# Loading wq with eight strided DMAs of 16 partitions in place of one DMA of 128, in a decode-step transformer block

## The chip, the cores and the metric

The kernel runs on one core of a Trainium2 chip. The metric is the device time of one execution in microseconds (us). Before the change the median of 3 runs is 203.08 us (203.05 to 203.18).

A core has five instruction streams. PE (TensorE) multiplies matrices, DVE (VectorE) and ACT (ScalarE) work element by element, POOL (GpSimd) builds constants here, and SP (SyncE) issues DMAs. A DMA moves bytes between device memory (HBM) and the on-chip buffer SBUF, which has 128 partitions (rows). Sixteen DMA engines share the work of each load. An instruction that needs a load waits on that load's semaphore.

## What is computed

One token goes through one transformer block: attention over a cache of 4096 positions with 32 heads of 128, then a gated MLP, each behind a layer norm and with a residual. All inputs are bf16.

```python
h  = x + A(layernorm(x))
h2 = h + B(layernorm(h))
# A: q = (x @ wq) as 32 heads of 128; scores = q . k_cache / sqrt(128); p = softmax(scores)
#    o = p . v_cache; result = o (4096 values) @ wo
# B: (gelu(x @ w_gate) * (x @ w_up)) @ w_down
# x: 640; wq: 640 x 4096; k_cache, v_cache: 32 x 4096 x 128; wo: 4096 x 640
# w_gate, w_up: 640 x 1728; w_down: 1728 x 640
```

Every weight and both caches are read once: 84.23 MB, of which the caches are 67.1 MB and wq is 5.24 MB.

## The kernel before, in words

**Program order.** The kernel is a list of operations for each engine, with the operations that each waits for written out by hand. `Prog.op` (line 50) appends one, `Prog.dma` (58) appends a DMA, `emit` (63) gives each DMA a semaphore of its own, which reaches 16 when the load has landed, and `_run` (90) writes the instructions with their waits. Each engine runs its list in order. `P.emit({"sync": 2})` (573) puts the first two operations of SP's list ahead of the barrier at which the engines meet at the start, so these two DMAs go out first; the rest of the list follows behind the barrier.

**The loads.** All long loads are issued by SP, in this order: wq (line 186), three cache loads (210), the other cache loads as their buffers come free, three loads of wo, and nine loads of w_gate, w_up and w_down (451 to 468). x alone (1.2 KB) comes from ACT's queue (185). Line 59 is the line of every DMA in the profile.

wq goes into the tile `arena`, 128 partitions of 20,480 elements. Its 640 rows are seen as 128 groups of five, `"(p c) n -> p (c n)"`, so partition p takes one run of 40,960 B from HBM. Later wo takes the same tile, when the q projection has read wq.

The caches come in 16 groups, K and V for G = 0 to 7, four heads each: 128 partitions of 32 KB, 4.19 MB. They go through three buffers (`slots`). Group n waits until the reader of group n - 3 is done (`consumed`, line 206). The last V group comes in two halves.

**The start.** POOL and DVE build constants while the first loads are in flight. x is turned into columns (line 252), normalized (258 to 267) into `xlnB`, and the q projection (line 280; the repeated matmuls have line 28, that of a helper) multiplies it with wq: 40 matmuls, all behind one wait for the whole of wq. The two halves of q are copied to `qb` by DVE (285) and ACT (286). q is needed by the first product on K.

**The groups.** For each group G and each quarter of its K tile, DVE multiplies K by q (`prod`, line 295), PE adds up the products in PSUM (305 and 28), DVE finishes the sums (313) and ACT takes the exponential (317). Then PE multiplies the V tile by these (336 and 28), and DVE and PE pick and collect the heads (353 to 369).

**The end.** The output projection with wo (404), the residual, the second layer norm, gate and up (509), gelu, and down (553), whose last matmuls wait for the last w_down load; four copies (566, 568) and one store.

The functions that the edit touches, with those that call them:

## Time and profile before

| what | us |
|---|---|
| median of 3 runs | 203.08 |
| the profiled execution | 202.97 |
| its span, first to last instruction | 201.7 |
| wq: issue to landing | 15.5 |
| K loads, eight of 4.19 MB: median from issue to landing | 21.0 |
| V loads, seven of 4.19 MB: median from issue to landing | 17.7 |
| first matmul on wq begins at | 15.66 |
| first product on K begins at | 25.25 |
| last load lands at | 199.06 |

How to read the views. All times are from the start of the span. "Busy" of an engine is the time in which it executed something. A row of digits gives the busy share of equal slices in tenths, 9 for 90% or more. The DMA row is the mean busy share of the 16 DMA engines; GB/s is what they moved, booked at the moment when a packet starts, so short slices show bursts. A packet is one row of a load (up to 40 KB here), or the few bytes that each engine writes at the end of its part to count the load's semaphore up. An issue of a DMA is an instruction on SP (SPq); its landing is when its semaphore is complete. Matmul ends are modelled.

### The profile page before, as it was taken

What the parts mean: (1) busy time and instruction counts of PE and PEld (TensorE: products, weight loads), DVE (VectorE), ACT (ScalarE), POOL (GpSimd) and SP (SyncE); (2) the same over time, 40 slices, a digit from 0 to 9 for tenths busy, and PEclk for the clock granted to TensorE, in tenths of its full rate; (3) what the DMA queues carried; (4) which work ended last, traced back from release to release, by engine and by line L of the source; (5) the groups of instructions that cost most, each with busy time, mean ns of one, the idle gap of its engine ahead of it and who ended that gap; (6) DMA issues with size and microseconds to landing.
All of it is one profiled execution on the core that took longest, in us unless ns stands there. A gap on an engine that the chain in (4) does not pass through costs nothing.

```text
span 201.7 us, 1568 instructions
## 1 busy us (share of the span) xinstructions
PE 115.3 (57%) x788; PEld 17.0 (8%) x384; DVE 129.5 (64%) x136; ACT 51.3 (25%) x139; POOL 5.6 (3%) x15
## 2 busy tenths in 40 slices
PE   0108059536737775197529655876396097754564
PEld 0101000000001000000000001001000000121222
DVE  1300188517994898379857966896879979683341
ACT  2100003610560055005502440252025214500111
POOL 7300000000000000000000000000000000000000
PEclk9999756996996699859997978798569859997575
DMA  9999999999999999999999999999999999999992
GB/s 333 439 398 455 442 422 416 416 442 468 432 422 416 416 422 455 443 442 417 416 416 445 442 448 422 422 416 429 442 442 448 387 429 423 427 409 439 415 408 99
DMA packets 4330, 84.32 MB, mean 418 GB/s; under 512 B 482, under 2 KB 868, under 8 KB 1508
## 3 DMA queue, kind: packets, MB, share of 16 engines
q1 hardware_dynamic: 4322, 84.23, 97.9%
q8 instruction: 4, 0.07, 0.1%
q14 instruction: 2, 0.02, 0.0%
q10 hardware_dynamic: 2, 0.00, 0.0%
HBM read 84.23 MB, written 0.00 MB: 418 GB/s over the span
## 4 chain that ended last, share of the span: by engine, by line
DMA 52%; DVE 21%; PE 19%; issue 3%; ACT 2%; SPq 2%
DMA slot<-in_A_k_cache_dram 43%; DVE prod L295 16%; PE bank L28 13%; DMA slot<-in_B_w_down_dram 9%; DVE sc L313 3%; PE bank L336 3%; PE bank L305 2%; ACT p_bd L317 2%; SPq L59 2%; DVE po_r L363 1%; DVE po_m L353 1%; PE bank L553 0%; DVE out_row L566 0%; DVE RT L349 0%; DVE aP L393 0%
## 5 line engine op out<-in xcount | busy, mean ns | idle before, releaser
L295 DVE TENSOR_TENSOR prod<-slot,qb 128x4096 bf16<-128x4096 bf16 x32 | 72.4, 2283 | 24.3 <-DMA slot<-in_A_k_cache_dram 24.3
L317 ACT ACTIVATE p_bd<-sc,zero_t 32x32 bf16<-32x32 f32 x128 | 46.4, 362 | 107.7 <-DVE sc L313 106.5
L28 PE MATMUL bank<-prod,id_b 128*128 128x512 bf16 x224 | 68.6, 458 | 0.0
L305 PE MATMUL bank<-prod,id_b 128*128 128x512 bf16 x32 | 15.3, 477 | 45.2 <-DVE prod L295 45.1
L313 DVE TENSOR_REDUCE sc<-bank 128x32 f32<-128x512 f32 x32 | 22.0, 687 | 14.7 <-PE bank L28 14.7
L336 PE MATMUL bank<-slot,p_bd 128*32 128x512 bf16 x128 | 14.8, 448 | 15.0 <-ACT p_bd L317 13.8
L28 PE MATMUL bank<-slot,p_bd 128*32 128x512 bf16 x128 | 14.9, 453 | 0.0
L305 PEld LDWEIGHTS bank<-prod,id_b 128*128 128x128 bf16 x32 | 3.5, 109 | 108.6 <-DVE prod L295 108.6
L363 DVE TENSOR_REDUCE po_r<-po_m 128x128 f32<-128x1024 f32 x6 | 11.2, 1867 | 0.0
L353 DVE TENSOR_TENSOR po_m<-bank,m 128x1024 f32<-128x1024 f32 x8 | 9.7, 1214 | 0.6 <-PE bank L28 0.6
L280 PE MATMUL bank<-arena,xlnB 128*32 128x512 bf16 x20 | 3.3, 628 | 7.2 <-DMA arena<-in_A_wq_dram 7.2
L285 DVE CAST qb<-bank 128x512 bf16<-128x512 f32 x1 | 0.7, 692 | 10.0 <-PE bank L28 10.0
L336 PEld LDWEIGHTS bank<-slot,p_bd 128*32 128x32 bf16 x128 | 3.8, 106 | 35.7 <-ACT p_bd L317 26.1
L509 PE MATMUL bank<-slot,hlnT 128*1 128x512 bf16 (+1 forms) x40 | 4.0, 486 | 2.7 <-DVE hX L500 2.2
L349 DVE TENSOR_REDUCE RT<-p_bd 128x4 f32<-128x512 bf16 x8 | 5.4, 675 | 0.0
L252 PE MATMUL bank<-one_bf,x_row 1*128 1x1 bf16 x5 | 0.4, 177 | 7.1 <-DMA x_row<-in_A_x_dram 7.1
L369 PE MATMUL bank<-po_r,hs 128*16 128x128 f32 x16 | 3.4, 301 | 1.5 <-DVE po_r L361 1.5
L286 ACT CAST qb<-bank 128x512 bf16<-128x512 f32 x1 | 0.6, 586 | 10.4 <-PE bank L28 10.4
L28 PE MATMUL bank<-arena,xlnB 128*32 128x512 bf16 x20 | 3.2, 613 | 0.0
L404 PE MATMUL bank<-arena,aP 128*1 128x320 bf16 x32 | 2.5, 314 | 1.1 <-DMA arena<-in_A_wo_dram 1.1
L263 ACT ACTIVATE ln<-ln,eps_t 128x1 f32<-128x1 f32 x2 | 0.6, 294 | 9.4 <-DVE ln L261 9.4
L482 ACT CAST A_hi<-bank 97x320 bf16<-97x320 f32 x1 | 0.4, 426 | 9.8 <-PE bank L28 9.8
(87 smaller groups left out, 42.9 us busy)
## 6 DMA issues: line engine op xcount, KB each, us to landing
slot<-in_A_k_cache_dram SPq DMA_DIRECT2D x8, 4096.0 KB, 21.0
slot<-in_A_v_cache_dram SPq DMA_DIRECT2D x7, 4096.0 KB, 17.7
arena<-in_A_wq_dram SPq DMA_DIRECT2D x1, 5120.0 KB, 15.5
slot<-in_A_v_cache_dram SPq DMA_DIRECT2D x2, 2048.0 KB, 14.9
arena<-in_A_wo_dram SPq DMA_DIRECT2D x1, 2560.0 KB, 22.9
slot<-in_B_w_gate_dram SPq DMA_DIRECT2D x1, 2160.0 KB, 11.0
arena<-in_A_wo_dram SPq DMA_DIRECT2D x1, 1920.0 KB, 27.0
slot<-in_B_w_up_dram SPq DMA_DIRECT2D x1, 1296.0 KB, 13.7
```

What stands on the lines that cost most here:

```text
L28: return e.add_instruction(mybir.InstMatmult(name=nc.get_next_instruction_name(), engine=e.engine, start_tensor_calc=start, stop_tensor_ca ...
L59: ev = self.op(eng, lambda e: e.dma_start(out, in_), *deps, dma=True)
L295: m = V(lambda e: e.tensor_tensor(out=prod[:, s % 4, :, :], in0=kt[:, 32 * u:32 * u + 32, :], in1=qb[:, G, :].unsqueeze(1).to_broadcast([1 ...
L305: i = e.matmul(*args, start=True, stop=False)
L313: reds[s] = V(lambda e: e.reduce_sum(sc[:, s % 4, :], ps_f[s % 2][:, :].rearrange("p (g d) -> p g d", d=16), axis=AX.X), folds[s], exps.ge ...
L317: x = A(lambda e, j=j: e.activation(p_bd[32 * j:32 * j + 32, G % 2, 32 * (s % 4):32 * (s % 4) + 32, j], sc[32 * j:32 * j + 32, s % 4, :], ...
L336: return e.matmul(*args, start=(c < 4), stop=(c >= 12))
L349: sums[G] = V(lambda e: e.reduce_sum(RT[:, 4 * G:4 * G + 4], p_bd[:, G % 2, :, :].rearrange("p g j -> p j g"), axis=AX.X), exps[4 * G + 3])
L353: mks[G] = V(lambda e: e.tensor_tensor(out=po_m[:, :, :], in0=po[:, :].rearrange("p (b d) -> p b d", b=8), in1=m8[:, :].unsqueeze(2).to_br ...
L363: evs[G] = V(lambda e: e.reduce_sum(po_r[:, G % 2, :], po_m[:, :, :].rearrange("p b d -> p d b"), axis=AX.X), mks[G], hds.get(G - 2))
L369: return e.matmul(ps_a[0:16, 128 * (G // 4):128 * (G // 4) + 128], hs[:, 12 - 4 * g:28 - 4 * g], po_r[:, G % 2, :], start=(g == 0), stop=( ...
L509: i = e.matmul(po[32 * a:32 * a + 1, 512 * k:512 * k + n], hlnT[:, c:c + 1], w[:, c, 512 * a:512 * a + n], start=(c == 0), stop=(c == 4))
```

## The change

One load of wq becomes eight. Load k takes the 16 partitions k, k + 8, k + 16, ... k + 120 of the same tile from the same rows of HBM, each still one run of 40,960 B. The eight are issued by SP in the order k = 0 to 7, in the place in which the one load stood, and the q projection waits for all eight. The two DMAs ahead of the start barrier are now the loads k = 0 and 1; the first cache load stands behind the barrier. No other operation changes; behind line 186 the line numbers grow by one.

```diff
     d_x = P.dma("scalar", x_row[:, :], A_x[0, :, :])
-    d_wq = [P.dma("sync", arena[:, :], A_wq[:, :].rearrange("(p c) n -> p (c n)", c=5))]
+    wq_v = A_wq[:, :].rearrange("(p c) n -> p (c n)", c=5)
+    d_wq = [P.dma("sync", arena[k:128:8, :], wq_v[k:128:8, :]) for k in range(8)]
     order = [(kind, G) for G in range(NG - 2) for kind in "KV"] + [(kind, G) for kind in "KV" for G in (NG - 2, NG - 1)]
```

## The prediction, made before the changed kernel ran

> **What bounds the kernel now.** I read the page first, for what is busy all the time.

> ```profile
> span 201.7 us, 1568 instructions
> PE 115.3 (57%) x788; PEld 17.0 (8%) x384; DVE 129.5 (64%) x136; ACT 51.3 (25%) x139; POOL 5.6 (3%) x15
> ...
> DMA  9999999999999999999999999999999999999992
> ...
> q1 hardware_dynamic: 4322, 84.23, 97.9%
> ```

> No compute engine passes 64%, while the 16 DMA engines work in every slice but the last; SP's queue alone fills 97.9% of them. The kernel is one stream of loads. Next I cut the span into stages, to see whether the stream has a gap anywhere (columns: stretch, its length, busy time of each engine, clock, DMA share, GB/s).

> ```profile
> 0.00:15.50 15.50, 0.95 (x7) 0.77 (x7) 2.46 (x14) 1.87 (x3) 5.59 (x15) 1.00 0.98 402
> 15.50:25.20 9.70, 4.35 (x40) 0.87 (x20) 0.69 (x1) 0.59 (x1) 0.00 (x0) 0.90 1.00 432
> 25.20:64.40 39.20, 25.12 (x130) 2.21 (x42) 26.55 (x20) 11.58 (x32) 0.00 (x0) 0.81 0.99 428
> ...
> 177.60:199.10 21.50, 11.97 (x191) 5.59 (x157) 8.68 (x29) 1.91 (x5) 0.00 (x0) 0.72 0.95 393
> 199.10:201.70 2.60, 0.70 (x16) 0.31 (x16) 0.63 (x2) 0.57 (x2) 0.00 (x0) 0.50 0.00 0
> ```

> There is none. After the last landing at 199.1 only 2.6 us are left, so whatever the stream loses comes out at the end in full. Does a freed slot ever hold up a load, so that a delay could be absorbed there? The page gives 21.0 us from issue to landing for the K loads and 17.7 for the V loads, where a 4.19 MB load by itself needs 4.19 / 0.433 = 9.7 us. So at every issue some 8 to 11 us of older loads are still ahead; SP is never late, and nothing in the middle can take up a delay.

> Last I look at the DMA part of the stretch in which wq alone is moving.

> ```profile
> DMA  9900399900399900399300799003999003999003
> GB/s 1560 624 0 0 156 936 936 473 0 0 156 1092 780 468 0 0 156 1092 1092 156 0 0 312 1560 624 0 0 156 936 936 468 0 0 156 1092 780 468 0 0 156
> DMA packets 113, 4.55 MB, mean 433 GB/s; under 512 B 1, under 2 KB 2, under 8 KB 2
> ...
> q1 hardware_dynamic: 111, 4.55, 100.0%
> ```

> This is 3.3 to 13.8 us in 40 slices. GB/s are booked where a packet starts, and they come in bursts seven times in 10.5 us, one each 1.5 us: the 16 engines start a row of 40 KB together, take 1.5 us over it, and start the next together. 40,960 B in 1.51 us is 27.1 GB/s for each engine and 433 for all. The same view of K and V loads (45 to 65 us, rows of 32 KB) has 437, of the weights (177 to 188 us, rows of 1.3 to 20 KB) 422. One rate for every row length and every tensor: the sources don't set it. What sets it is either the engine's own speed or the way into SBUF that it writes through. In this kernel each long load covers all 128 partitions, so the trace can't tell the two apart, and on that the prediction turns.

> **The change part by part.**

> *Bytes and rows.* 128 rows of 40 KB stay 128 rows of 40 KB: 5.243 MB, or 5.243 / 0.433 = 12.1 us of the stream. Nothing is removed.

> *Issues on SP.* Seven are added. The trace has 0.33 to 0.61 us for one. The first two instructions of SP go out ahead of the start barrier: until now wq at 0.00 and K0 at 0.44, now wq's first two loads. The other six follow from 1.26 us, at 0.43 each until 3.9, and K0, V0 and K1 move from 0.44, 1.26 and 1.64 to about 3.9, 4.3 and 4.7. Each load of wq keeps the engines for 1.5 us, over three times its issue; the third goes out at 1.26 and is needed at 4.8, and K0 is needed at 13.9. Cost 0, hidden by the rows in flight; were an issue to take longer than a row, the stream would stand still for the difference at each of the six. No other instruction of SP waits for anything new.

> *Completion packets.* The page counts 482 packets under 512 B, 16 for each of SP's 30 big loads and 2 more; now 7 × 16 = 112 are added. No view prices one by itself. Nothing is the lower bound: 45 to 65 us holds 32 of them and runs at 437, wq's stretch holds one and runs at 433. Upper bound: the stretch 177 to 188 has 75 and loses 3% of 11 us against 437, 0.4 us, so 0.6 us for 112 if all of that were theirs. I take 0.1, near the first row, which has the long rows that wq has too.

> *Waits.* PE's first wq matmul waits for eight loads in place of one. Its weights are ready at 10.08 us and wq at 15.66, so the waits lie in idle time of PE, and only the last landing counts. Queued behind are PE's folds, and they wait for K0 (25.2) anyway: from wq's landing to both halves of q takes 5.1 us (15.66 to 20.74), leaving 4.5 us. If wq is late, K0 in the same queues is late by as much, and the 4.5 stays. x lands at 7.08 between rows of wq; with rows of 3 us it may come some 5 us later and the weights at 15, still ahead of wq.

> *Where the rows go.* This is the one large term. Until now a load names all 128 partitions. Each new load names sixteen, k, k + 8, ... k + 120, and as all engines run in step, these sixteen are written at the same time, for k = 0 to 7 in turn. If the engines' own speed is the limit, the price is 0. If it is the ways into SBUF, and numbers eight apart come back to the same ways, then two rows share one and each goes at half of 27.1 GB/s: wq needs 24.2 us in place of 12.1, 12.1 more. If four share, it is 36.3 more. On the side of gains there is next to nothing, since no stretch of the trace is above 437. I take the half: full rate is shown here for the spread over 128 partitions alone, the stream is deaf to everything on the side of the source, and a comb with teeth eight apart is regular enough to meet any regular share-out of partitions over ways unevenly; of the unequal outcomes two on one way is the mildest. 0 and +12.1 are the ends that I keep for the range. One deduction: by the DMA view of 0.9 to 4.1 us the first rows start spread over 0.8 us (1.0 to about 1.8), and while only one of two sharers is running it has the full rate; half of that spread, 0.4 us, comes off.

> [...]

> **Sum.** 12.1 − 0.4 + 0.1 = +11.8 us. The profiled execution took 202.97 (span 201.7 and 1.3 around it), 0.1 under the median of 203.08; 202.97 + 11.8 = 214.8, or 214.9 on the median. I give **214.8**, with 213.3 to 215.8 if only this case's terms are off.

> **Rivals.**

> *Not slower: the engine is the limit, or each row goes to the engine that already owns its way.* Then wq's last row still lands at 15.5, eight issues hide as above, and the time stays 203.1. For it: the row time of 1.51 us is so even that a fixed engine speed explains it well. It needs no sharing at all; the deciding point is whether a row of the first loads takes 1.5 us or 3.0. [...] I give it 0.15, 0.02 of that for a gain above 0.2% (0.4 us, what a measurement of this kernel can tell from no change).

> [...]

> [...]

> *More than double.* Four rows on one way, or losses at each change between two rows: up to +36.3, 239. 0.04.

> **Chances.** Forecast 0.73, not slower 0.15, half 0.08, more 0.04. Faster by over 0.2%: 0.02; within: 0.13; slower: 0.85. The range goes from the half price (209.0, less 0.2) to the top of the forecast, 208.8 to 216.0, and holds 0.81.

> **What would show it.** In the DMA view of wq's stretch: bursts 3.0 us apart and a mean near 217 GB/s, with the DMA share still near 1 (a packet that waits for its way counts as busy). PE's first wq matmul at about 27.4 in place of 15.66, DVE's first product at 37.0 in place of 25.25, later stages as long as before, the last landing near 210.9 and 2.6 us behind it. Bursts 1.5 us apart and K0 at 25.2 would prove the forecast wrong; gaps in the DMA share between the loads would mean that the issues or the completions cost what I put at nothing.

## The result, and the profile after

The changed kernel takes 216.59 us (median of 6 runs, 216.4 to 216.8) against 203.11 for the kernel before on the same chip: a ratio of 1.066, 95% interval 1.0646 to 1.0674, or 13.5 us more. The profiled execution took 216.64, 13.7 more than the one before it was compared with. The forecast was 214.8 with a range to 216.0: the right side and the right mechanism, but 1.8 us too little, and outside the range.

The page of the kernel after, the 40 slices of DMA share and GB/s (5.4 us each), and then the stages, cut where its own landings are (columns as before):

```profile
DMA  9899899999999999999999999999999999999992
GB/s 236 175 198 243 195 383 420 432 438 414 456 414 441 420 444 420 426 450 415 444 415 447 414 420 456 414 450 414 450 420 426 444 402 434 422 412 429 413 412 99
```

```profile
0.00:28.00 28.00, 0.95 (x7) 0.77 (x7) 2.47 (x14) 1.87 (x3) 5.59 (x15) 1.00 0.97 206
28.00:38.00 10.00, 4.46 (x40) 0.86 (x20) 0.69 (x1) 0.59 (x1) 0.00 (x0) 1.00 1.00 429
38.00:78.00 40.00, 23.73 (x130) 2.22 (x42) 26.36 (x19) 11.58 (x32) 0.00 (x0) 0.91 1.01 432
...
191.00:212.80 21.80, 12.49 (x207) 5.99 (x167) 9.24 (x30) 1.91 (x5) 0.00 (x0) 0.74 0.94 387
212.80:215.40 2.60, 0.64 (x16) 0.26 (x16) 0.63 (x2) 0.57 (x2) 0.00 (x0) 0.50 0.00 0
```

Nearly all of the loss is in the first stage; 0.9 us more comes between the first K load and the third, and the part on the prediction returns to it. In the first stage the DMA engines are busy as before (0.97), but they move 206 GB/s where they moved 402; from the first K load (K0) on the stream has its old rate (429 and 432 GB/s), and the 2.6 us behind the last landing are still 2.6. A DMA share near 1 is no proof of a full stream: here 0.97 stands beside 206 GB/s, for an engine counts as busy to the end of its row, however long that takes (3.17 us against 1.51). The DMA view of the stretch in which wq alone moves, 3.3 to 26 us in slices of 0.57 us:

```profile
DMA  9999309993009993099930999930999300999307
GB/s 217 217 433 217 72 0 219 433 433 72 0 0 433 433 217 72 0 217 289 577 72 0 217 217 433 217 72 0 217 433 433 72 0 0 433 433 217 72 0 173
DMA packets 232, 4.69 MB, mean 207 GB/s; under 512 B 116, under 2 KB 117, under 8 KB 117
...
q1 hardware_dynamic: 230, 4.69, 99.5%
```

The bursts are 5.6 slices apart, 3.2 us, where they were 1.5. Sixteen rows of 40 KB at 207 GB/s take 655 KB / 207 = 3.17 us. In the timeline, what hangs on wq moves by 13.1 us (15.66 before) and K0 by 12.9 (25.25 before):

```profile
28.73 0.62 PE L281 MATMUL bank<-arena,xlnB 128*32 128x512 bf16 x4 [18.56 <-DMA arena<-in_A_wq_dram]
...
38.11 4.49 DVE L296 TENSOR_TENSOR prod<-slot,qb 128x4096 bf16<-128x4096 bf16 x2 [4.18 <-DMA slot<-in_A_k_cache_dram]
```

### The profile page after: what moved, and what is told of

Its sections match the earlier page's. It is cut to its first block, busy times and chain, and to the rows that moved or that the text cites. A ratio compares the mean times of both kernels' runs of the same rounds, so it can differ in the third digit from the quotient of the medians.

```text
span 215.4 us, 1578 instructions
## 1 busy us (share of the span) xinstructions
PE 114.9 (53%) x788; PEld 17.0 (8%) x384; DVE 129.6 (60%) x136; ACT 51.3 (24%) x139; POOL 5.6 (3%) x15
## 3 DMA queue, kind: packets, MB, share of 16 engines
q1 hardware_dynamic: 4434, 84.23, 97.7%
HBM read 84.23 MB, written 0.00 MB: 391 GB/s over the span
## 4 chain that ended last, share of the span: by engine, by line
DMA 52%; DVE 20%; PE 19%; issue 4%; SPq 3%; ACT 2%
DMA slot<-in_A_k_cache_dram 44%; DVE prod L296 15%; PE bank L28 13%; DMA slot<-in_B_w_down_dram 8%; PE bank L337 3%; SPq L59 3%; DVE sc L314 3%; PE bank L306 2%; ACT p_bd L318 2%; DVE po_r L364 1%; DVE po_m L354 1%; PE bank L554 0%; DVE out_row L567 0%; DVE RT L350 0%; DVE aP L394 0%
## 5 line engine op out<-in xcount | busy, mean ns | idle before, releaser
L28 PE MATMUL bank<-prod,id_b 128*128 128x512 bf16 x224 | 67.5, 452 | 0.0
L306 PE MATMUL bank<-prod,id_b 128*128 128x512 bf16 x32 | 15.2, 477 | 46.5 <-DVE prod L296 46.3
L314 DVE TENSOR_REDUCE sc<-bank 128x32 f32<-128x512 f32 x32 | 22.0, 687 | 13.8 <-PE bank L28 13.8
L337 PE MATMUL bank<-slot,p_bd 128*32 128x512 bf16 x128 | 15.2, 462 | 15.0 <-ACT p_bd L318 13.8
L28 PE MATMUL bank<-slot,p_bd 128*32 128x512 bf16 x128 | 15.2, 462 | 0.0
L364 DVE TENSOR_REDUCE po_r<-po_m 128x128 f32<-128x1024 f32 x6 | 11.2, 1868 | 0.0
L264 ACT ACTIVATE ln<-ln,eps_t 128x1 f32<-128x1 f32 x2 | 0.6, 296 | 10.5 <-DVE ln L262 10.5
## 6 DMA issues: line engine op xcount, KB each, us to landing
slot<-in_A_v_cache_dram SPq DMA_DIRECT2D x7, 4096.0 KB, 18.8
```

Source lines behind the costliest of these rows:

```text
L28: return e.add_instruction(mybir.InstMatmult(name=nc.get_next_instruction_name(), engine=e.engine, start_tensor_calc=start, stop_tensor_ca ...
L306: i = e.matmul(*args, start=True, stop=False)
L314: reds[s] = V(lambda e: e.reduce_sum(sc[:, s % 4, :], ps_f[s % 2][:, :].rearrange("p (g d) -> p g d", d=16), axis=AX.X), folds[s], exps.ge ...
L337: return e.matmul(*args, start=(c < 4), stop=(c >= 12))
L364: evs[G] = V(lambda e: e.reduce_sum(po_r[:, G % 2, :], po_m[:, :, :].rearrange("p b d -> p d b"), axis=AX.X), mks[G], hds.get(G - 2))
```

## The experiments

Three theories stood at the start. **Shared ways**: rows in flight together share the rate of a way into SBUF when their partitions lie on the same one. **Narrow loads**: many small loads, one row for each engine, are slow by themselves. **Source**: rows read 320 KB apart are slow to read. All times are medians beside runs of the kernel before on the same chip (203.10 to 203.17). The diffs are against the changed kernel, two of them, as said there, against the kernel before.

### Eight loads, but all partitions in each

```diff
-    d_wq = [P.dma("sync", arena[k:128:8, :], wq_v[k:128:8, :]) for k in range(8)]
+    d_wq = [P.dma("sync", arena[:, 2560 * k:2560 * (k + 1)], wq_v[:, 2560 * k:2560 * (k + 1)]) for k in range(8)]
```

> wq in eight loads of all 128 partitions, 2,560 columns each (rows of 5,120 B). Three theories of the 13.5 us. Shared ways: rows that are in flight together and whose partitions lie on the same way into SBUF share its rate; all 128 partitions in each load, so wq takes 12.1 us as before and the time is 203.1 to 203.7 (1,024 short rows in place of 128 long ones may cost some tenths). Narrow loads: many loads with their own issues and completions are slow by themselves; eight loads here too, 216 or at least several us over 203.1. Source: rows read 320 KB apart are slow to read; rows here are 40 KB apart as before, 203.1.

Measured: 203.69, ratio 1.0025 (1.0016 to 1.0035). Eight issues, eight sets of completions and eight waits cost half a microsecond together with the short rows, not 13.

### Sixteen neighbours

```diff
-    d_wq = [P.dma("sync", arena[k:128:8, :], wq_v[k:128:8, :]) for k in range(8)]
+    d_wq = [P.dma("sync", arena[16 * k:16 * k + 16, :], wq_v[16 * k:16 * k + 16, :]) for k in range(8)]
```

> wq in eight loads of 16 partitions next to each other (0 to 15, 16 to 31, ...). Shared ways: if a way serves four neighbouring partitions, the sixteen rows in flight lie on four ways, four on each; a row takes 4 x 1.51 = 6.1 us or a little more (the pairs took 3.17 where 3.03 is half rate), wq 48 to 51 us, the time 239 to 242. Narrow loads: 216.6, as with the sixteen rows eight apart. Source: the rows are neighbours in HBM, 203.1. [...]

Measured: 236.25, ratio 1.1638 (1.1619 to 1.1658), 33.1 us more. The DMA view, 3.3 to 46 us:

```profile
DMA packets 240, 4.82 MB, mean 113 GB/s; under 512 B 120, under 2 KB 121, under 8 KB 121
```

A quarter of 433 would be 108. Same number and size of loads as the change, only other partitions with the rows that belong to them, and 20 us slower still: narrow loads and source both fail here. On the size, shared ways missed: it had 36 to 39 us more. The trace has a record of every packet, with its start and length; by these a row took 5.7 us behind the first, not 6.1.

### Two halves

```diff
-    d_wq = [P.dma("sync", arena[k:128:8, :], wq_v[k:128:8, :]) for k in range(8)]
+    d_wq = [P.dma("sync", arena[64 * k:64 * k + 64, :], wq_v[64 * k:64 * k + 64, :]) for k in range(2)]
```

> wq in two loads, partitions 0 to 63 and 64 to 127. Shared ways: 216 (203.1 + 13) if 64 neighbouring partitions reach only half of the ways; 203.1 if the ways are spread evenly over neighbours. Narrow loads: only two loads, four rows for each engine in each, 203.1 to 203.5. Source: 203.1. [...] If it is slow, the row time tells the rest: 3.03 us would put the 0.14 us above half rate down to the completion behind each row, 3.17 to the sharing itself.

Measured: 216.56, ratio 1.0663 (1.0645 to 1.0681). The DMA view, 3.3 to 26 us:

```profile
DMA packets 132, 4.62 MB, mean 204 GB/s; under 512 B 18, under 2 KB 19, under 8 KB 19
```

Two loads cost the same as eight: the number of loads is next to nothing here, the partitions are nearly everything. And the rate is as far under half as in the change, so the completion behind each row isn't what lies between 3.03 and 3.17.

### Same partitions, rows that are neighbours in HBM

```diff
-    d_wq = [P.dma("sync", arena[k:128:8, :], wq_v[k:128:8, :]) for k in range(8)]
+    d_wq = [P.dma("sync", arena[k:128:8, :], wq_v[16 * k:16 * k + 16, :]) for k in range(8)]
```

> The eight loads as in the change (partitions k, k + 8, ...), but load k reads rows 16 k to 16 k + 15 of wq, which are neighbours in HBM; partition p therefore gets another row of wq than the matmul takes it for, so q is computed from permuted rows, with the same work. Shared ways: 216.6, as the change. Narrow loads: 216.6. Source: 203.1, or at least several us under 216.6.

Measured: 216.19, ratio 1.0646 (1.063 to 1.0662). The pattern of the reads has at most 0.4 us in it at this rate; whether it would hold up a faster stream, this run doesn't say.

### Sixteen rows, seven apart

```diff
-    d_wq = [P.dma("sync", arena[k:128:8, :], wq_v[k:128:8, :]) for k in range(8)]
+    d_wq = [P.dma("sync", arena[k:k + 106:7, :], wq_v[k:k + 106:7, :]) for k in range(7)]
+    d_wq.append(P.dma("sync", arena[112:128, :], wq_v[112:128, :]))
```

> Eight loads of sixteen rows again, but seven of them take partitions k, k + 7, ... k + 105 (k = 0 to 6) and the last takes 112 to 127. Shared ways, with the ways as the runs so far bound them (four neighbours on one way, 0 to 63 apart from 64 to 127, eight apart two on one way): most rows of a load of step 7 are alone on their way. Each engine's eight rows worked through with halves and quarters where they meet give 18.2 us for the slowest engine in place of 12.1: 6.1 more, 208.5 to 210.5. Narrow loads: one row for each engine and eight completions as in the change, 216.6.

Measured: 215.42, ratio 1.06 (1.0581 to 1.062): a miss by 5 us. The view of 3.8 to 22 us has the six loads of step 7 behind the first, and the last load, the one of sixteen neighbours:

```profile
DMA packets 226, 4.59 MB, mean 252 GB/s; under 512 B 113, under 2 KB 114, under 8 KB 114
```

The trace doesn't show ways, and the runs so far leave open which rows of these loads meet. Up to 18.8 us, where only loads of step 7 move, the same view gives 262 GB/s, and by the packet records all sixteen rows of the second load were slow alike, 2.7 to 3.0 us each. If each way slowed only those that meet on it, most rows would take 1.5 us by the author's estimate; the working that gave the expected 18.2 us has some 360 GB/s for these six loads, an estimate too. Then either a meeting holds up engines that have no part in it, or the narrow loads are slow after all, or a row is slower over a way that is another engine's in a load of 128. The last two kernels below were made to tell these apart.

### 32 rows four apart, and 64 rows two apart

```diff
-    d_wq = [P.dma("sync", arena[k:128:8, :], wq_v[k:128:8, :]) for k in range(8)]
+    d_wq = [P.dma("sync", arena[k:128:4, :], wq_v[k:128:4, :]) for k in range(4)]
```

> wq in four loads of 32 rows, partitions k, k + 4, ... k + 124. Each load reaches all ways with two rows each, two rows for each engine. What it tells apart is how rows are dealt to engines. Dealt in the order of the rows, two in a row: engine i writes partition 8 i + k, then 8 i + k + 4, and all engines in step make the pattern of the change, 216.6. Dealt by the way that a row goes to, as the load of 128 must be (in the order of the rows, that one would have the pattern of the change, too, and it runs at full rate): 203.1 to 203.7. [...]

Measured: 203.52, ratio 1.0018 (1.0009 to 1.0028). The DMA view of 3.3 to 13.8 us has the old picture, bursts 1.5 us apart:

```profile
DMA  7997007997009993009990009990079970099930
GB/s 312 1248 624 312 0 0 312 1248 629 312 0 0 780 780 780 156 0 0 1248 780 468 0 0 0 1248 780 468 0 0 312 1248 624 312 0 0 780 780 780 156 0
DMA packets 162, 4.59 MB, mean 437 GB/s; under 512 B 49, under 2 KB 50, under 8 KB 50
```

```diff
-    d_wq = [P.dma("sync", arena[k:128:8, :], wq_v[k:128:8, :]) for k in range(8)]
+    d_wq = [P.dma("sync", arena[k:128:2, :], wq_v[k:128:2, :]) for k in range(2)]
```

> wq in two loads of 64 rows, the even and the odd partitions. Each load reaches all ways, four rows for each engine. Dealt in the order of the rows, engine i writes 8 i, 8 i + 2, 8 i + 4, 8 i + 6 (and k): two rows on one way at all times, 216.6. Dealt by ways: 203.1 to 203.6. With the loads of 0 to 63 and 64 to 127 (216.56) it says whether 64 rows are slow as such or by which partitions they are.

Measured: 203.44, ratio 1.0013 (1.0004 to 1.0023). So 64 rows cost 13 us as 0 to 63 and 64 to 127, and 0.3 as even and odd. It also shows that rows aren't dealt to the engines in runs of neighbours, since that would have been the pattern of the change, 216.59.

### The same split on another load, late in the stream

Against the kernel before:

```diff
-    wo_load("0", 0, 0, 16)
+    wo_v = A_wo[0:2048, :].rearrange("(p i) n -> p i n", i=16)
+    d_wo["0"] = P.dma("sync", wo_sb[0:64, 0, :, :], wo_v[0:64, :, :], qd)
+    d_wo["0b"] = P.dma("sync", wo_sb[64:128, 0, :, :], wo_v[64:128, :, :], qd)
```

> wq in one load as before; the first load of wo (2.62 MB, 128 rows of 20 KB, late in the stream) in two, partitions 0 to 63 and 64 to 127. Shared ways: the price goes with the bytes, wherever they are in the stream: eight rows for each engine at 3.17 / 2 = 1.585 us in place of 0.757, 6.6 more, 209.7 (209.2 to 210.2). If the price of the change came from the start of the kernel (cold first rows, the barrier, the issue order), nothing of it would be here: 203.1.

Measured: 210.86, ratio 1.0379 (1.0364 to 1.0395), 7.7 us more. The price isn't one of the start; it goes with the bytes, at 2.9 us per MB here and 2.6 for wq. It is 0.7 us over what was expected at most, and the packet records show where the rest lies. On the mean of the engines the eight rows of the split load took 12.4 us in place of 6.2, but the next load of wo took 5.7 in place of 4.6 and the V load ahead 10.1 in place of 9.8: the loads on either side of the half-rate rows paid too.

### More work for eight of the sixteen engines

Against the kernel before:

```diff
+    d_wq.append(P.dma("sync", prod[0:32:4, :, :, :].rearrange("p a b d -> p (a b d)"),
+                      A_wq[0:32, :].rearrange("(p a) n -> p (a n)", a=4)))
```

> wq in one load as before; behind it one more load of eight rows of 32 KB (rows of wq again, to partitions 0, 4, ... 28 of a tile that is not yet in use), which only eight of the sixteen engines can take, one row each: 1.21 us more for these eight, nothing for the others. Latest engine: each engine has its own list and none takes over another's rows, so the end moves by what the latest engine gets. Of the two that are late in before, one begins 1.3 us behind and one loses 1.6 us to an instruction fetch; if either is among the eight, the time grows by up to 1.2 (204.3), if neither, by some 0.1 to 0.2. Evening out: the engines share the bytes, 0.26 MB / 433 GB/s = 0.6, 203.7.

Measured: 204.26, ratio 1.0054 (1.004 to 1.0068): 1.1 us, nearly the 1.21 of one row, and more than the 0.6 of shared bytes. The engines don't even out; the latest one sets the end. The shift shows late, 0.3 us at the landing of the third K load and 1.2 at the last landing (200.22 against 199.06).

### Sixteen rows, each on a way of its own

```diff
-    d_wq = [P.dma("sync", arena[k:128:8, :], wq_v[k:128:8, :]) for k in range(8)]
+    d_wq = [P.dma("sync", arena[k:k + 61:4, :], wq_v[k:k + 61:4, :]) for k in (32, 33, 34, 35)]
+    d_wq += [P.dma("sync", arena[k:k + 31:2, :], wq_v[k:k + 31:2, :]) for k in (0, 1, 96, 97)]
```

> Eight loads of sixteen rows once more: the first four take partitions k, k + 4, ... k + 60 for k = 32 to 35, the last four 0, 2, ... 30; 1, 3, ... 31; 96, ... 126; 97, ... 127. By the ways as the runs bound them, the first four put each of their sixteen rows on a way of its own, and the last four put two on each of eight. Shared ways: bursts 1.5 us apart for the first four loads, 3.2 us apart for the last four; 4 x 1.51 + 4 x 3.17 = 18.7 us for wq, 6.6 more than before, 209.4 to 210.2. Narrow loads: all eight alike, 216.6. [...]

Measured: 211.11, ratio 1.0386 (1.0364 to 1.0408). Two stretches of one kernel decide it: 3.4 to 6.4 us, in the first four loads, and 8 to 20, in the last four.

```profile
DMA packets 64, 1.31 MB, mean 437 GB/s; under 512 B 31, under 2 KB 32, under 8 KB 32
```

```profile
DMA  0996660009999069000099966900009996096000
GB/s 0 1092 683 137 137 137 0 0 0 273 683 546 273 0 137 273 0 0 0 0 546 546 546 137 137 273 0 0 0 0 546 546 546 137 0 273 137 0 0 0
DMA packets 128, 2.62 MB, mean 218 GB/s; under 512 B 64, under 2 KB 64, under 8 KB 64
```

In the second, the bursts are ten slices of 0.3 us apart, 3.1 us for a row: loads of sixteen rows run at 437 or at some 210, by their partitions alone. Narrow loads are out. Which of the two patterns gives each row a way of its own was the author's estimate ahead of the run; the trace agrees with it. The total is 0.9 us over what was expected at most. The first product on K is 7.0 us later than before (32.24), so the last microsecond of the 8.0 comes behind K0, as it does in the change (see "Why the prediction was off").

### Eight rows at a time, nothing else moving

```diff
-    d_wq = [P.dma("sync", arena[k:128:8, :], wq_v[k:128:8, :]) for k in range(8)]
+    d_wq = [P.dma("sync", arena[a:a + 29:4, :], wq_v[a:a + 29:4, :])
+            for a in (0, 1, 2, 3, 32, 33, 34, 35, 64, 65, 66, 67, 96, 97, 98, 99)]
...
-            landed[n] = [P.dma("sync", dst[:, i * w:(i + 1) * w], src[:, i * w:(i + 1) * w], consumed[n - NSLOT] if n >= NSLOT else None)
+            landed[n] = [P.dma("sync", dst[:, i * w:(i + 1) * w], src[:, i * w:(i + 1) * w], *([consumed[n - NSLOT]] if n >= NSLOT else d_wq))
```

A foreign way is one that is another engine's in a load of 128. By the two halves (204 GB/s each, all 128 together 433) partitions 0 to 63 and 64 to 127 lie on different ways. If an engine has one way in a load of 128, which no run shows, then for one that writes to both, at least one of the two is foreign.

> wq in sixteen loads of eight rows, four partitions apart, which eight engines alone take; first those of partitions 0 to 63, then those of 64 to 127, and the first cache load is held back until all of wq has landed, so that nothing else is moving. [...] It is to tell why the loads of step 7 were slow (215.42 where 18.2 us for wq and 210 were expected). If a foreign way is as good as the own one: bursts 1.5 us apart all through, 216 GB/s, wq landed at about 26 and 215 to 217 in all, and the slowness of step 7 comes from meetings alone, which then hold up engines beyond the two that meet. If a foreign way is slower by itself: bursts 1.9 to 2.9 us apart in the last eight loads, 219 to 227.

Measured: 218.5, ratio 1.0745 (1.0724 to 1.0765). The view of 15 to 25 us, in slices of 0.25 us, when the rows of partitions 64 to 127 move:

```profile
DMA  3039333039333039333037930337930309930309
GB/s 164 0 164 655 164 164 164 0 164 655 164 164 164 0 164 655 164 164 164 0 164 328 492 164 0 164 164 328 492 164 0 164 0 492 492 164 0 164 0 492
DMA packets 104, 2.13 MB, mean 213 GB/s; under 512 B 52, under 2 KB 52, under 8 KB 52
...
q1 hardware_dynamic: 104, 2.13, 49.5%
```

Bursts six slices apart, 1.5 us, at half of the engines: 213 GB/s for eight is 27 for each, the full rate, just as in the first eight loads (3 to 13 us, also 213). SP had issued all sixteen loads by 11.5 us, and the rate didn't rise; so the same eight engines took both lots. Neither a foreign way nor one row for each load slows an engine down when eight of them move. Of the three explanations of step 7 one is left: a meeting on one way holds up engines that go elsewhere. That is argued by exclusion, and no run shows the meeting itself, or which rows of the loads of step 7 meet. Two rivals weren't run: all sixteen engines on foreign ways at once with no meeting, and rows 280 KB apart in HBM at a rate above half (the source was varied only under the half rate of the change). That the time is above the 215 to 217 expected lies in the hold: K0, issued at 28.25 behind wq's landing, is used first at 40.51, 12.3 us later, of which its rows are 9.7.

## Why the prediction was off

By its own steps:

- **Bound.** Right. What the stream lost at the start came out at the end: +13.1 at wq, +13.6 at the last landing, 13.7 in the span.
- **Where the rows go.** The choice of "half" was right, its size wasn't. **This is the term of the sum that failed**: it stood at 12.1 − 0.4 = 11.7 us and came to 12.8. The numbers that follow are means over the sixteen engines, from the packet records of the two profiled executions; the trace doesn't number the engines, so each packet is put to the engine whose last packet ended just before it.
  - The step took two rows on one way to go at exactly half of 27.1 GB/s, 3.03 us for a row. Rows two to eight of wq took 3.14 us (six of them 3.15 to 3.19, one 2.98; the 207 GB/s of the view makes 3.17), 11.4 us more than before for the seven, where the prediction has 10.6.
  - The first rows of wq took 2.96 us in place of 2.32. That is 0.6 more, where the prediction has 1.51 less the deduction of 0.4, 1.1.
  - The first rows of K0 took 1.96 us in place of 1.21, 0.75 more. The prediction has nothing for this: it lets wq end at one time, but the engines were done with it between 25.8 and 27.8 us, and the early ones wrote rows of K0 beside the last slow rows of wq. That these met on a way is likely and not shown by a run of its own; the load behind the split load of wo paid in the same manner.
- **Issues on SP.** Put at 0, "hidden by the rows in flight". True of all but the first, ahead of which nothing is in flight. The issue of one such load takes longer, and the first row starts later, at 1.35 us in place of 1.0:

```profile
L59 SPq DMA_DIRECT2D arena<-in_A_wq_dram x8: 498/582/589, 0.0 to 4.9; - x8
```

(Shortest, median and longest issue in ns; the one load of before took 382.) The price is 0.35 us, 0.37 on the mean of the engines. The two kernels with combs at full rate (32 rows four apart, 64 rows two apart) show it nearly alone: their issues have medians of 566 and 575 ns, and they are 0.4 and 0.3 us slower than before.
- **Completion packets** at 0.1, **waits** at 0: nothing in the runs speaks against either. The gaps between an engine's rows of wq grew by 0.04 us in all. q had 4.5 us to spare before K0 and has 4.2.

With these, 12.8 + 0.4 = 13.2 us, and by 13.25 the engines are later on the mean at the end of K0 (13.3 at the end of the third K load, K2). What is left, up to 13.8 at K2 and 13.6 at the last landing, goes by which engine is the latest. The traces show this at K2, and no term of the prediction has it.

K0 landed 12.9 us later, less than that mean, and K2 13.8 later, more. The chain of waits has a landing of a K load in both kernels, before and after, and there the ends of K0, K2 and K4 (the fifth K load) can be read:

```profile
0.44 24.78 DMA slot<-in_A_k_cache_dram
...
43.21 21.16 DMA slot<-in_A_k_cache_dram
...
81.50 21.72 DMA slot<-in_A_k_cache_dram
```

```profile
5.55 32.53 DMA slot<-in_A_k_cache_dram
...
57.20 20.97 DMA slot<-in_A_k_cache_dram
...
96.07 20.96 DMA slot<-in_A_k_cache_dram
```

Start and length in us: K0 landed at 25.22 before and 38.08 after; K2 at 64.37 and 78.17, 13.80 apart; K4 at 103.22 and 117.03, 13.81 apart. Between K0 and K2 the DMA view has one packet of another queue in each kernel, an instruction fetch; these lines are from the views of 44.7 to 64.4 us before and of 57.6 to 68.7 us after:

```profile
q8 instruction: 1, 0.02, 0.3%
```

```profile
q8 instruction: 1, 0.02, 0.6%
```

It goes over one of the sixteen engines and puts that one behind by 1.5 us (by the packet records its eight rows around the fetch took 11.2 us in both kernels, those of other engines 9.7), and it is still behind at K4. The landings of K0 and K2 are 0.37 to 0.47 us behind the end of the rows on the latest engine. At the end of K0 in before that was an engine that had begun late (the lone 156 GB/s behind each burst in the prediction's DMA view), 1.26 us behind the engine that gets the fetch (24.85 and 23.59). In after, the latest engine was only 0.31 behind the one that gets it (37.65 and 37.34). From K2 on the latest is the engine with the fetch, in both kernels: 63.90 and 77.74 at the end of K2's rows, 13.8 apart, where the mean of the engines is 13.3. K0 to K2 took 39.15 before, 40.09 after, 40.07 and 39.67 with the combs of 32 and of 64 rows, but 39.05 with more work on eight engines, while K2 to K4 took 38.9 in all but that one (39.2). That this engine is the reason is read from the traces; no run moved the fetch.

Of the rivals: "not slower" is the fate of other combs (32 rows by four, 64 by two), not of this one; "half the price" and "four on one way" are wrong for sixteen eight apart, and the second is what sixteen neighbours do (113 GB/s). The 209.0 of the half price, from which the range begins, takes sharers that fall out of step half way, which no run shows: in the change, rows two to eight of wq took 3.14 us, the eighth as long as the second.

## What to carry to other kernels

## What the runs showed of the hardware beyond that

- Two rows on a way, as the sixteen eight apart are taken to lie, are a little worse than half (207 GB/s; on eight ways, 25.9 each, with 27.1 alone), four, as the sixteen neighbours are, are better than a quarter (113; on four ways, 28.3 each). The numbers of ways are an estimate from these rates and the 433. The rows of pairs took 3.17, 3.20 and 3.17 us (medians) in the change, the halves and the run with neighbours in HBM; fours were run in one kernel, 5.68 us for a row. The reason is open.
- In the loads of step 7 the whole stream fell to 262 GB/s, 61% of 433, though most rows of a load are alone on their way by the working that gave the expected 18.2 us, an estimate. That a meeting holds up those who don't meet is what is left by exclusion, with the two rivals above not run.
- The deal of rows to engines isn't by neighbours: a load of 128 ran at 433 GB/s, 32 combed by four at 437, and with 64 combed by two the kernel took 0.3 us more than before (203.44).
- The engines keep their lateness to the end: one extra row of 1.21 us on eight of them, 0.3% of the bytes, cost 1.1 us, and a fetch that puts one engine behind by 1.5 us sets the landings behind it.
